# Two decode layers on one core: the last half row of the second up projection in two loads, and nine idle products less

## The chip, the cores and the metric

The kernel runs on 1 core of one Trainium2 chip. The metric is the device time of one execution in microseconds (us); the kernel before takes 2681.52 us, median of 3 runs (2681.52 to 2681.58). The names of the engines are those of the profile: PE multiplies matrices (PEld loads its stationary operand), DVE, ACT and POOL work on vectors, SP does nothing here but issue transfers, and 16 DMA engines carry them from the memory into `space`, the one large buffer on the core. Idle products are matmuls whose results nobody reads; they only keep PE occupied.

## The reference

Two tokens (B = 2) go through the same attention block and the same gated MLP twice. Cut to what matters:

```python
def _A_ref(x, k_cache, v_cache, wq, wo):           # H = 32 heads of 128, 8192 cached keys, all float32
    q = (x @ wq).reshape(B, 1, H, 128).transpose(0, 2, 1, 3)
    p = softmax(einsum("bhqd,bhkd->bhqk", q, k_cache) * 128 ** -0.5)
    o = einsum("bhqk,bhkd->bhqd", p, v_cache)
    return o.transpose(0, 2, 1, 3).reshape(B, 1, H * 128) @ wo      # wo: 4096 x 576
def _B_ref(x, w_gate, w_up, w_down):               # 576 -> 4608 -> 576
    h = gelu(x @ w_gate) * (x @ w_up)
    return h @ w_down
x = A_x
for _ in range(2):
    x = x + _A_ref(layernorm(x), A_k_cache, A_v_cache, A_wq, A_wo)
    x = x + _B_ref(layernorm(x), B_w_gate, B_w_up, B_w_down)
```

The caches are 268 MB each and are read once for each layer; a few units stay on the core between the layers.

## The kernel before, in words

**Order of the loads.** `plan_first`, `plan_mlp(0)`, `plan_second` and `plan_mlp(1)` put every load of the program into one list, and `pump` issues them in that order on SP as soon as the place in `space` that a load wants is free. A load is freed by `done(key)` after the last instruction that reads it. So SP's queue has one fixed order, and a load that waits for its place holds back all behind it.

**Attention** walks over 34 items (two heads of one token, or one head at the end): DVE multiplies keys and query, POOL and DVE add up, ACT takes the exponentials, PE multiplies with the values. Layer 1 walks backwards over the items, so that what lies on the core at the end of layer 0 is used first. At the end of an attention `project(g)` multiplies with pieces of `wo`.

**MLP.** In layer 0 (`split`) the three weights come in pieces of 1152 KB through a ring of four places (`RING`, `NPLACE`), each piece multiplied by `split_products` or by the loop over `DOWN` and freed at once. In layer 1 they come in few large pieces that are put wherever there is room (`Arena.fit`). There a weight of 576 x 4608 is looked at as 1152 half rows of 2304 numbers (9216 bytes); partition p holds the half rows 9p to 9p + 8, and half row number `u` of every partition is called the `u`-th. `half_rows` loads a range of `u` for all 128 partitions. `GU` says which ranges make a load: gate 0 to 4 and 5 to 8, up 0 to 5 and 6 to 8. The ninth half row is `u` = 8.

**The matching x.** `norm` turns the normalised x into `xt`: 32 columns for each `u`, of which two, at `PAD + 32 * u`, hold x for the full row, and the two behind them hold x for the other half; the rest is zero. `window(u, at)` takes eight columns, so that a product of eight columns lands gate and up, and both halves, in rows of their own in `acc`. `all_products` multiplies: for each `u` two halves of the columns and four groups, eight matmuls, each of 288 columns. In float32 the profile shows each matmul as two.

**Behind it** `activate` (ACT and DVE) makes gelu(gate) * up, the loop over `DOWN[1]` multiplies with the five pieces of `w_down`, `add_to_x` adds, and two transfers store x.

**Idle products.** `idle_products(n, side)` writes matmuls of the identity into a part of PSUM that is free just then: two of 128 columns without a side and for n = 1, one of 512 columns with a side and n = 2. `IDLE` gives their numbers ahead of each piece of `DOWN`; others stand between the pieces of `wo` at the end of the first attention.

Of the kernel before, what the change touches and what calls it, by code (L numbers as in the profile page):

```python
# [15 lines left out]
P = 128  # L16
B = 2
# [8 lines left out]
HALF = P // 2  # L26
# [3 lines left out]
NU = 9  # L30
EQ = 512
HG = DF // 16
PAD = 6
NT = 4
NI = DF // (NT * P)
CW = D // 4
# [89 lines left out]
def decode_layers(ctx, tc, x_in, kc, vc, wq, wo, wg, wu, wd, out):  # L126
    nc = tc.nc
# [21 lines left out]
    queue, ready, places = [], {}, {}  # L149
# [5 lines left out]
    def done(key):  # L155
        arena.free(key)
        pump()
# [93 lines left out]
    def half_rows(key, w, us, first):  # L251

        width = w.shape[1] // 2
        rows = w.rearrange("r (s w) -> (r s) w", w=width).rearrange("(p u) w -> p u w", p=P)

        def transfers(t):
            nc.sync.dma_start(t.rearrange("p (u w) -> p u w", w=width), rows[:, us[0]:us[-1] + 1, :])

        weights(key, len(us) * width, first, transfers)

    def of_half(h, k):

        width = wq.shape[1] // 2
        rows = wq.rearrange("r (s w) -> (r s) w", w=width).rearrange("(m u) w -> m u w", u=2 * NU)
        first, step = (2 * k + h, NU + 1 - 2 * h)

        def transfers(t):
            nc.sync.dma_start(t, rows[:, first:first + step + 1:step, :])

        weights(("wq", 1, h, k), width, None, transfers)  # L270
# [54 lines left out]


    single = [range(u, u + 1) for u in range(NU)]
    GU = [[range(0, 5), range(5, NU)], [range(0, 6), range(6, NU)]]

    DOWN = [  # L330
        [[(h, lo, lo + 4)] for h in range(2) for lo in range(0, 16, 4)] + [[(h, 16, 18) for h in range(2)]],
        [[(0, 0, 18)]] + [[(1, lo, hi)] for lo, hi in ((0, 9), (9, 15), (15, 17), (17, 18))],
    ]

    IDLE = [(0, 0, 2, 0, 2, 0, 2, 0, 0), (10, 2, 2)]

    whole_at = (None, 0)
    def groups(layer):
        return range(H // WIDE[layer])[::1 - 2 * layer]
# [76 lines left out]
    def plan_mlp(layer):  # L416
        if layer == 0:
            for h in range(2):
                for u in range(4):
                    split_rows("g", wg, h, u)  # L420
                for u in range(4):
                    split_rows("u", wu, h, u)
                if h == 0:
                    split_ninth("g", wg)
                    split_ninth("u", wu)
        else:
            for g, (name, w) in enumerate((("g", wg), ("u", wu))):
                for us in GU[g]:
                    half_rows((name, layer, us[0]), w, us, 0)
        for piece in DOWN[layer]:  # L430
            down(layer, piece)

# [99 lines left out]
    def small(p, n):  # L532

        if n > 2:
            return turned[0:p, 0:n]
        return pair[0:p, 0:n]
# [50 lines left out]
    def idle_products(n, side=None):  # L587
        wide = P if side is None else 4 * P if n % 2 == 0 else 2 * P
        to = turned if side is None else acc[:, side, :wide]
        for _ in range(2 * P * n // wide):  # L590
            nc.tensor.matmul(
                to[0:4, :], ident[:, 0:4], ident.unsqueeze(1).to_broadcast([P, wide // P, P]), start=True, stop=True
            )
# [13 lines left out]
    def attention(layer):  # L607
# [30 lines left out]
        else:  # L638
            half_products(1)
            key = ("wq", 1, NU - 1)  # L640
# [434 lines left out]
        if layer == 0:  # L1075
            project(second)

            third, fourth, fifth = groups(layer)[2:5]
            values(N - 1, 0, 2)
            for g in (third, fourth):  # L1080
                project(g)
                idle_products(1)
            for k in range(2, ITEMS[n].parts, 2):
                values(N - 1, k, k + 2)
                if k + 2 == ITEMS[n].parts:
                    nc.scalar.copy(back, spare)
                idle_products(1)
            gather(n)
            project(fifth)
            idle_products(1)  # L1090
            context(n)
            divide(n)
        else:
            values(N - 1)
            finish(n)
            regroup()
        spread()
        for g in groups(layer)[5:] if layer == 0 else groups(layer):
            project(g)
            if layer == 0 and g != groups(layer)[-1]:  # L1100
                idle_products(1)
        add_to_x()


    def mlp(layer):
# [10 lines left out]
        def split_products(h):  # L1116
# [3 lines left out]
            for key, u, g in steps:  # L1120
# [10 lines left out]
                if key != steps[-1][0]:  # L1131
                    idle_products(1, 1 - h if (u < 4 if h == 0 else u) else None)

        def all_products():

            for g, name in enumerate("gu"):
                for us in GU[g]:
                    w = ready.pop((name, layer, us[0])).rearrange("p (u c m v i) -> p u v c m i", m=32, v=2, c=4, i=NI)
                    for u in us:
                        for v in range(2):  # L1140
                            for c in range(4):
                                nc.tensor.matmul(
                                    acc[32 * c:32 * c + 4 * B, v, :HG], window(u, 4 * g), w[:, u - us[0], v, c],
                                    start=(g == 0 and u == 0), stop=(g == 1 and u == NU - 1),
                                )
                    done((name, layer, us[0]))

        def activate(v):

# [19 lines left out]
                nc.vector.scalar_tensor_tensor(to[:, :, s, :], a, 1.0, by, op0=ALU.add, op1=ALU.mult)  # L1169

        if not split:
            all_products()
        for v in range(2):
            if split:
# [54 lines left out]
```

## Time and profile before

| what | us |
|---|---|
| median of 3 runs | 2681.52 |
| the profiled execution's own time | 2681.31 |
| its span, first to last instruction | 2679.5 |
| PE, DVE, POOL, ACT busy | 880.8, 1992.6, 1560.5, 165.7 |
| bytes read | 1152.39 MB, 430 GB/s over the span |

The 1.8 us between the span and the execution's time lie outside all instructions. Layer 0 ends at about 1367 us of the span, layer 1 takes the rest. A window row gives, for a stretch of the span, the busy time of the engines with the number of their instructions, the granted share of PE's clock, the mean busy share of the 16 DMA engines and the rate at which they moved bytes. (A share may be a little over 1, since a packet of an engine starts a few ns before the one ahead of it has ended.) In the chain of waits each row is a start, a length and what the program waited for.

### The profile page before, as it was taken

Reading aid. Unit: us, or ns where it says so; the run is one execution under the profiler, and the core shown is the slowest. Engines: PE = TensorE matmul, PEld = TensorE weight load, DVE = VectorE, ACT = ScalarE, POOL = GpSimd, SP = SyncE. Lnnn points to the kernel's source line nnn. Section 1 sums busy time; section 2 is a strip of 40 time slices with the busy share of each in tenths; the row PEclk is TensorE's granted clock in tenths of the full one; section 3 lists DMA queues with packets and bytes.
Section 4 is the critical chain, followed back from the end, with each engine's and each line's share of the span. In section 5 each row is a group of like instructions: output and inputs, shape, how many; then the busy total and the mean of one; then the engine's idle time right before and its main releaser. Section 6 shows DMA issues by size and latency. Waiting matters only on the chain.

```text
span 2679.5 us, 15405 instructions
## 1 busy us (share of the span) xinstructions
PE 880.8 (33%) x6198; PEld 268.7 (10%) x6198; DVE 1992.6 (74%) x907; ACT 165.7 (6%) x792; POOL 1560.5 (58%) x411
## 2 busy tenths in 40 slices
PE   1313332232223233334663323223222323332346
PEld 0000000000000000011221000000000000000022
DVE  4877888888788888867038778888888888888740
ACT  0000000000000000001026000000000000000000
POOL 2546676667667666744028457666766666676620
PEclk8666655665665566566986665566566556655678
DMA  9999999999999999999999999999999999999998
GB/s 423 437 429 434 436 434 432 431 436 433 431 434 434 434 433 432 436 428 427 417 417 431 436 433 434 434 430 434 435 432 432 436 434 433 431 437 434 428 430 385
DMA packets 29207, 1153.39 MB, mean 430 GB/s; under 512 B 3256, under 2 KB 3280, under 8 KB 4048
## 3 DMA queue, kind: packets, MB, share of 16 engines
q1 hardware_dynamic: 29096, 1152.40, 99.8%
q8 instruction: 48, 0.79, 0.1%
q14 instruction: 23, 0.19, 0.0%
q10 hardware_dynamic: 40, 0.01, 0.0%
HBM read 1152.39 MB, written 0.00 MB: 430 GB/s over the span
## 4 chain that ended last, share of the span: by engine, by line
DMA 67%; DVE 19%; PE 8%; POOL 2%; ACT 2%; issue 1%; another core or an unknown queue 0%; SPq 0%; POOLq 0%; ACTq 0%; DVEq 0%
DMA space<-in_A_k_cache_dram 59%; DVE space L743 17%; PE acc L891 3%; DMA space<-in_B_w_down_dram 2%; DMA space<-in_B_w_gate_dram 2%; POOL space L772 2%; DVE scores L775 2%; PE bank L658 1%; DMA space<-in_A_v_cache_dram 1%; DMA space<-in_B_w_up_dram 1%; PE bank L809 1%; ACT prz L832 1%; PE acc L913 1%; DMA space<-in_A_wo_dram 1%; PE bank L845 1%
## 5 line engine op out<-in xcount | busy, mean ns | idle before, releaser
L772 POOL TENSOR_TENSOR space<-space 128x3072 f32<-128x3072 f32 (+4 forms) x221 | 1128.4, 5106 | 459.1 <-DVE space L743 330.7
L743 DVE TENSOR_TENSOR space<-space,bank 128x6144 f32<-128x6144 f32 (+4 forms) x223 | 1111.9, 4987 | 344.7 <-DMA space<-in_A_k_cache_dram 273.7
L775 DVE TENSOR_REDUCE scores<-space 128x48 f32<-128x3072 f32 (+4 forms) x223 | 568.7, 2550 | 92.1 <-POOL space L772 92.1
L913 PE MATMUL acc<-space,prz 128*16 128x512 f32 (+1 forms) x3312 | 510.1, 780 | 357.9 <-DMA space<-in_A_v_cache_dram 346.4
L883 POOL TENSOR_TENSOR space<-space 128x2048 f32<-128x2048 f32 x147 | 398.0, 2708 | 392.3 <-DVE space L880 376.8
L658 PE MATMUL bank<-qsb,few 4*64 4x128 f32 (+1 forms) x256 | 46.1, 436 | 894.8 <-DVE space L743 887.1
L880 DVE TENSOR_TENSOR space<-space,bank 128x4096 f32<-128x4096 f32 x49 | 216.6, 4421 | 1.7
L913 PEld LDWEIGHTS acc<-space,prz 128*16 128x16 f32 (+1 forms) x3312 | 108.7, 117 | 742.0 <-issue 449.7
L824 ACT ACTIVATE nbs<-bank 128x2 f32<-128x2 f32 (+1 forms) x68 | 11.6, 171 | 2010.4 <-PE bank L809 1957.1
L658 PEld LDWEIGHTS bank<-qsb,few 4*64 4x64 f32 (+1 forms) x256 | 20.6, 201 | 914.2 <-DVE space L743 897.4
L580 POOL TENSOR_TENSOR rstd<-ve,few 128x1 f32<-128x1 f32 x4 | 2.2, 551 | 171.3 <-DVE ve L578 171.3
L891 PE MATMUL acc<-space,few 128*16 128x512 f32 x98 | 92.6, 1048 | 0.0
L801 PE MATMUL bank<-ident,m 128*1 128x128 f32 x68 | 20.7, 305 | 196.1 <-DVE m L799 195.9
L936 PE MATMUL bank<-few,wide 128*32 128x4 f32 (+1 forms) x272 | 20.9, 200 | 170.1 <-DVE wide L928 170.1
L1153 DVE STREAM_TRANSPOSE gu<-acc 128x288 f32<-128x288 f32 x4 | 1.9, 484 | 92.6 <-ACT acc L1151 92.6
L832 ACT ACTIVATE prz<-scores,nbs 64x128 f32<-64x128 f32 (+1 forms) x128 | 50.7, 396 | 11.7 <-POOL prz L822 8.9
L765 ACT ACTIVATE space<-space 128x128 f32<-128x128 f32 x164 | 48.4, 297 | 19.5 <-DVE space L743 16.5
L809 PE MATMUL bank<-m,few 1*128 1x2 f32 (+1 forms) x136 | 39.0, 353 | 28.1 <-DVE m L807 28.1
L584 DVE TENSOR_TENSOR x<-bank,x 128x144 f32<-128x144 f32 x4 | 1.2, 308 | 59.4 <-PE bank L1186 39.7
L927 DVE TENSOR_TENSOR acc<-acc,few 128x512 f32<-128x512 f32 x34 | 23.5, 691 | 29.2 <-PE acc L913 29.2
L936 PEld LDWEIGHTS bank<-few,wide 128*32 128x32 f32 x272 | 19.1, 154 | 216.0 <-issue 211.0
L955 ACT ACTIVATE oT<-bank,rinv 32x8 f32<-32x8 f32 x108 | 28.1, 260 | 190.1 <-PE bank L936 189.1
(105 smaller groups left out, 495.8 us busy)
## 6 DMA issues: line engine op xcount, KB each, us to landing
space<-in_A_v_cache_dram SPq DMA_DIRECT2D x7, 4096.0 KB
space<-in_A_k_cache_dram SPq DMA_DIRECT2D x6, 4096.0 KB
space<-in_B_w_gate_dram SPq DMA_DIRECT2D x9, 1152.0 KB
space<-in_B_w_up_dram SPq DMA_DIRECT2D x9, 1152.0 KB
space<-in_B_w_down_dram SPq DMA_DIRECT2D x8, 1152.0 KB
space<-in_A_wq_dram SPq DMA_DIRECT2D x9, 1024.0 KB
space<-in_A_wo_dram SPq DMA_DIRECT2D x2, 4608.0 KB
space<-in_A_k_cache_dram SPq DMA_DIRECT2D x4, 2048.0 KB
```

What stands on the lines that cost most here:

```text
L658: nc.tensor.matmul(qb[n][to, :], pick[32 * c:32 * c + 4, r:r + 1].to_broadcast([4, P // it.heads]), qsb[32 * c:32 * c + 4, (h % 4) * DH:(h ...
L743: nc.vector.tensor_tensor(out=u[:, :r, :], in0=t[:, :r, :], in1=qb[n].unsqueeze(1).to_broadcast([P, r, DH]), op=ALU.mult)
L765: nc.scalar.activation(u[:, j, :], u[:, j, :], AF.Copy, accum_out=S[n][:, base(n, k) + j:base(n, k) + j + 1])
L772: nc.gpsimd.tensor_tensor(out=half, in0=half, in1=u[:, :r, DH // 2:], op=ALU.add)
L775: nc.vector.tensor_reduce(out=S[n][:, base(n, k):base(n, k) + own_rows(n, k, m)], in_=prod.pop((n, k)), axis=AX.X, op=ALU.add)
L809: nc.tensor.matmul(mT[n][:, :heads], ones[0:1, :], m1[:, :heads], start=True, stop=True)
L832: nc.scalar.activation(pr[at, lo:].rearrange("p (g e) -> p g e", e=4)[:, 0:it.rows // 2 * it.heads:2 * it.heads, :], s[at, :it.rows].rearr ...
L880: nc.vector.tensor_tensor(out=t, in0=t, in1=share.unsqueeze(2).to_broadcast([P, rows, DH]), op=ALU.mult)
L883: nc.gpsimd.tensor_tensor(out=t[:, :rows - less], in0=t[:, :rows - less], in1=t[:, less:rows], op=ALU.add)
L891: nc.tensor.matmul(accumulator(n)[0:16, :], owner[:, 8 * ITEMS[n].b:8 * ITEMS[n].b + 16], part_at(arena.live[key, lo][0], 4 * DH), start=F ...
L913: nc.tensor.matmul(accumulator(n)[32 * c:32 * c + m, :], pr[:, at:at + m], t[g // 4][:, g % 4 * 4:g % 4 * 4 + 4, :].rearrange("p j d -> p ...
L936: nc.tensor.matmul(po[lo:lo + 32, i, :c], t[:, i::GH], of[:, :c], start=True, stop=True)
```

## The change

The ninth half rows of the second layer's up weight no longer come with the range 6 to 8. They come in two loads of 64 half rows each, behind the range 0 to 5. The half rows of the even partitions go to their own partitions, 0, 2, 4 and so on. Those of the odd partitions go to partitions 0 to 63, in a column range beside: the source is written as 8 x 8 rows with the outer step over `g`, so that row `j * 8 + g` of the 64 lands on partition `g * 8 + j`. To fit this, `spread_ninth` makes a permutation matrix from the identity (ACT), multiplies it with the ninth columns of `xt` (PE), and puts the permuted and the remaining x into unused zero columns of the ninth block (ACT). `ninth_products` multiplies both loads: eight matmuls over 128 partitions and eight over 64, instead of eight over 128. Nine idle products fall away: six of 128 columns at the end of the first attention and three of 512 columns ahead of pieces of the first `w_down`.

```diff
+NINTH = PAD + 32 * (NU - 1)
...
+    def ninth_rows(key, w):
+
+        width = w.shape[1] // 2
+        rows = w.rearrange("r (s w) -> (r s) w", w=width).rearrange("(q e u) w -> e q u w", e=2, u=NU)[:, :, NU - 1, :]
+        lower = rows[1].rearrange("(j g) w -> g j w", g=8)
+
+        def transfers(t):
+            nc.sync.dma_start(t[0:P:2, :width], rows[0])
+            nc.sync.dma_start(t[:HALF, width:], lower)
+
+        weights(key, 2 * width, 0, transfers)
...
-    GU = [[range(0, 5), range(5, NU)], [range(0, 6), range(6, NU)]]
+    GU = [[range(0, 5), range(5, NU)], [range(0, 6), range(6, NU - 1)]]
...
-    IDLE = [(0, 0, 2, 0, 2, 0, 2, 0, 0), (10, 2, 2)]
+    IDLE = [(), (10, 2, 2)]
...
             project(fifth)
-            idle_products(1)
             context(n)
...
         for g in groups(layer)[5:] if layer == 0 else groups(layer):
             project(g)
-            if layer == 0 and g != groups(layer)[-1]:
-                idle_products(1)
...
+        def spread_ninth():
+
+            perm = scores[:, :HALF]
+            nc.scalar.copy(
+                perm.rearrange("p (g j) -> p g j", g=8), ident.rearrange("p (j g e) -> p e g j", g=8, e=2)[:, 1]
+            )
+            moved = small(HALF, 2 * B)
+            nc.tensor.matmul(moved, perm, xt[:, NINTH:NINTH + 2 * B], start=True, stop=True)
+            nc.scalar.copy(xt[:HALF, NINTH + 24:NINTH + 24 + 2 * B], moved)
+            nc.scalar.copy(xt[:, NINTH + 12:NINTH + 12 + B], xt[:, NINTH:NINTH + B])
+
+        def ninth_products():
+
+            w = ready.pop(("u", layer, NU - 1)).rearrange("p (u c m v i) -> p u v c m i", m=32, v=2, c=4, i=NI)
+            for at, p in ((NINTH + 12, P), (NINTH + 24, HALF)):
+                for v in range(2):
+                    for c in range(4):
+                        nc.tensor.matmul(
+                            acc[32 * c:32 * c + 4 * B, v, :HG], xt[:p, at - 2 * B:at + 2 * B], w[:p, p == HALF, v, c],
+                            start=False, stop=False,
+                        )
+            done(("u", layer, NU - 1))
...
         if not split:
+            spread_ninth()
             all_products()
```

On SP, at the end of the second layer, the loads stand so before, a row with its partitions and the numbers in each:

```order
L320 DMA space<-in_A_wo_dram 128x9216 x2
L257 DMA space<-in_B_w_gate_dram 128x11520
L257 DMA space<-in_B_w_gate_dram 128x9216
L257 DMA space<-in_B_w_up_dram 128x13824
L257 DMA space<-in_B_w_up_dram 128x6912
L297 DMA space<-in_B_w_down_dram 128x10368
```

and now so:

```order
L258 DMA space<-in_B_w_gate_dram 128x9216
L258 DMA space<-in_B_w_up_dram 128x13824
L269 DMA space<-in_B_w_up_dram 64x2304
L270 DMA space<-in_B_w_up_dram 64x1x2304
L258 DMA space<-in_B_w_up_dram 128x4608
L310 DMA space<-in_B_w_down_dram 128x10368
```

The load of 128 x 6912 has become one of 128 x 4608 behind two of 64 x 2304; nothing passes anything else. (Line numbers differ because the file grew.)

On PE, in the second MLP, from the layer norm (`apart`) to the first piece of `w_down` (`hT`), before:

```order
L547 MATMUL bank_124<-apart,wide 128x24
L1142 MATMUL acc<-space,xt 8x288 x144
L591 MATMUL acc<-ident 4x512 x5
L1186 MATMUL bank<-space,hT 4x144 x72
L591 MATMUL acc<-ident 4x512
```

and now:

```order
L562 MATMUL bank_124<-apart,wide 128x24
L1153 MATMUL bank_124<-xt,scores 64x4
L1177 MATMUL acc<-space,xt 8x288 x120
L1163 MATMUL acc<-space,xt 8x288 x16
L1177 MATMUL acc<-space,xt 8x288 x16
L606 MATMUL acc<-ident 4x512 x5
```

One permuting product stands ahead, and sixteen products with the ninth half rows stand where eight stood, now ahead of the half rows 6 and 7.

On PE, in the first layer, from the last products with `w_up` (`xt`) over the first `w_down` (`hT`) to the norm of the second layer, before:

```order
L1125 MATMUL acc<-space,xt 8x288 x8
L1186 MATMUL bank<-space,hT 4x144 x32
L591 MATMUL acc<-ident 4x512
L1186 MATMUL bank<-space,hT 4x144 x32
L591 MATMUL acc<-ident 4x512
```

and now:

```order
L606 MATMUL acc<-ident 4x256
L1137 MATMUL acc<-space,xt 8x288 x8
L1224 MATMUL bank<-space,hT 4x144 x144
L606 MATMUL acc<-ident 4x256
L562 MATMUL bank_124<-apart,wide 128x24
```

The first lists the beginning of this `w_down`, with two of the three idle products in it; in the second all 144 matmuls of the nine pieces stand in one row. At the end of the first attention the same happens to the pieces of `wo`: the six idle matmuls between them are gone, and the real products stand in the same order.

More of the change, by code (lines that the diff above doesn't have):

```diff
@@ L429, in plan_mlp @@
                     half_rows((name, layer, us[0]), w, us, 0)
+                    if (g, us[0]) == (1, 0):
+                        ninth_rows((name, layer, NU - 1), w)
         for piece in DOWN[layer]:
@@ L1143, in all_products @@
                                     acc[32 * c:32 * c + 4 * B, v, :HG], window(u, 4 * g), w[:, u - us[0], v, c],
-                                    start=(g == 0 and u == 0), stop=(g == 1 and u == NU - 1),
+                                    start=(g == 0 and u == 0), stop=(g == 1 and u == NU - 2),
                                 )
                     done((name, layer, us[0]))
+                    if (g, us[0]) == (1, 0):
+                        ninth_products()
         def activate(v):
```

## The prediction

> **What bounds the kernel.** I read the page first, then the end of the chain of waits, then the last microseconds in windows.
>
> ```profile
> PE 880.8 (33%) x6198; PEld 268.7 (10%) x6198; DVE 1992.6 (74%) x907; ACT 165.7 (6%) x792; POOL 1560.5 (58%) x411
> ...
> DMA packets 29207, 1153.39 MB, mean 430 GB/s; under 512 B 3256, under 2 KB 3280, under 8 KB 4048
> ...
> 2622.76 46.63 DMA space<-in_B_w_down_dram
> ...
> 2669.43 2.39 PE bank L1186 x72
> ...
> 2673.56 2.57 PE bank L1186 x72
> ...
> 2676.16 0.31 DVE x L584
> ```
>
> No compute engine is busy for more than 74%. The DMA engines carry 430 GB/s over the whole span, and the chain ends with a load of `w_down` that waited 46.6 us behind other loads. So the end is set by when the last DMA engine has carried its share; PE follows within a microsecond. The question is whether all 16 end together:
>
> ```profile
> 2670.00:2670.50 0.50, 0.50 (x24) 1.00 1.03 424
> 2670.50:2671.00 0.50, 0.50 (x24) 1.00 0.84 346
> 2671.00:2671.50 0.50, 0.50 (x24) 1.00 0.65 272
> 2671.50:2672.00 0.50, 0.50 (x13) 1.00 0.60 253
> 2672.00:2672.50 0.50, 0.50 (x2) 1.00 0.54 221
> 2672.50:2673.00 0.50, 0.16 (x1) 1.00 0.71 268
> 2673.00:2673.50 0.50, 0.00 (x0) 1.00 0.53 217
> 2673.50:2674.00 0.50, 0.44 (x16) 1.00 0.40 161
> 2674.00:2674.50 0.50, 0.50 (x24) 1.00 0.46 180
> 2674.50:2675.00 0.50, 0.50 (x24) 1.00 0.18 69
> 2675.00:2675.50 0.50, 0.50 (x23) 1.00 0.01 5
> ```
>
> These are PE's windows; the last two numbers are the DMA share and the rate. They do not end together. The share falls like a staircase from 2670.5 to about 2675.1 (0.01 of the last window on 16 engines is 0.08 us on one). Times 16 it counts the engines still at work: 10 in the window from 2671.0, 8.5 in that from 2673.0, 6.4 in that from 2673.5. The sum of the ten shares from 2670.5 on is 4.92; times 0.5 us the mean engine ends 2.46 us after 2670.5, at 2672.96. Perfect balance would thus save 2675.1 - 2673.0 = 2.1 us, 0.08% of the time. No way of dealing out the same bytes at the end can save more.
>
> **The two loads.** The ninth half rows are 128 packets of 9216 bytes. Before, as part of 128 rows, each of 16 engines carries 8 of them. How a load of fewer rows is dealt out, the start and the whole program show (first 100 us, then the page):
>
> ```profile
> q10 hardware_dynamic: 32, 0.01, 0.0%
> ...
> x<-in_A_x_dram ACTq DMA_DIRECT2D x8, 1.1 KB
> ...
> q1 hardware_dynamic: 29096, 1152.40, 99.8%
> ```
>
> Eight loads of two rows make 32 packets: 16 rows, and two closing packets for each load, so each row had an engine of its own. SP's 202 loads of 128 rows and one store of four make 29096 = 202 x (128 + 16) + 8 packets: sixteen engines for 128 rows, four for four. A load thus spreads over up to 16 engines by its outer count. That of the even half rows (outer 64) should go to 16, four rows each. That of the odd ones is written with an outer count of 8 and should go to 8, eight rows each. Then eight engines carry 12 rows and eight carry 4, where all carried 8: four rows, 36.9 KB, are moved from each of one half to each of the other. At 431 GB/s (below), 26.9 for one engine, that is 1.37 us later for one half and 1.37 us earlier for the other. Eight engines also get 8 smaller packets for 8 large ones. The price of more packets is bounded by two stretches, small packets in the first, 64 KB in the second:
>
> ```profile
> 1250.00:1370.00 120.00, 78.52 (x1061) 32.39 (x1061) 20.17 (x47) 3.35 (x12) 7.35 (x7) 0.91 1.01 419
> ...
> 2480.00:2580.00 100.00, 32.23 (x193) 0.62 1.00 431
> ```
>
> 9216 bytes take 352 ns at 419/16 and 342 ns at 431/16, so at most 10 ns for a packet, 0.1 us for eight and the closing ones.
>
> Whether 1.37 us is gained or lost depends on which half is late. Of that I know only this: something delays single engines.
>
> ```profile
> q8 instruction: 7, 0.11, 0.5%
> ```
>
> In the last 100 us seven packets of instructions, 16 KB each, took 0.5% of 1600 engine-us: 8 us, 1.1 us for each, every one on one engine. Four on one engine and none on another make the staircase. No view names engines; the packets followed from end to start put these fetches on eight engines alone, and the two that load x at the start are not among them. If the eight of the odd load are the first eight, as those two would be, the late half is relieved. I take that.
>
> Then the late half ends at 2675.1 - 1.37 = 2673.7. The early half ended by about 2673.5, where the count falls below eight, and ends at 2674.9 at most now. So the early half sets the new end: a gain of 0.2 us at the row's edge, 0.7 us if its last engine was done at 2673.0. The count there is still 8.5, so I stay near the edge: 0.3 us, less 0.1 us for the packets, 0.2 us. Both ends are kept: -1.4 us if the early half is earlier than the rows let it seem, +1.5 us if the late half gets the bytes.
>
> [...]
>
> **Work that is added in the second MLP**, all of it beside transfers:
>
> ```profile
> 2608.44 0.69 DVE L574 STREAM_TRANSPOSE xt<-xc 128x288 f32<-128x288 f32 x1
> ...
> 2615.62 7.11 PE L1142 MATMUL acc<-space,xt 128*8 128x288 f32 x80 [8.08 <-DMA space<-in_B_w_gate_dram]
> ...
> 2642.79 11.60 PE L1142 MATMUL acc<-space,xt 128*8 128x288 f32 x144 [10.58 <-DMA space<-in_B_w_up_dram]
> ...
> 2654.52 0.47 ACT L1151 ACTIVATE acc<-acc,rstd 128x288 f32<-128x288 f32 x1 [80.27 <-PE acc L1142]
> ...
> 2657.39 5.86 PE L591 MATMUL acc<-ident 128*4 128x512 f32 x10 [3.00 <-DVE gu L1153]
> ...
> 2669.43 2.39 PE L1186 MATMUL bank<-space,hT 128*4 128x144 f32 x72 [0.74 <-DMA space<-in_B_w_down_dram]
> ...
> 2620.62 8.28 SPq L297 DMA_DIRECT2D space<-in_B_w_down_dram  x5
> ```
>
> The permutation is three ACT copies (0.47 us each at most, by the far larger row) and one PE product: 1.5 us with hand-overs. ACT idles 80 us there, the first copy needs nothing of the norm, and PE waits 8.08 us for the gate weight, 6.5 us of it after `xt` is there at 2609.1. Cost nothing; with that cover gone, 1.5 us. Eight more matmuls show as 16; at 11.60/144 = 81 ns that is 1.3 us. They push `activate` and the 5.86 us of idle products back, and the first products with `w_down` by as much; ahead of the second piece PE idles 0.74 us behind another 1.02 us of idle products, which is the cover. Cost nothing; without the cover 1.3 us. The larger place for the ninth rows makes the third to fifth `w_down` pieces wait for the second gate load's products (about 2632) in place of the first's (2622.8). On the way to the end they have 30 us and more of loads ahead of them (46.63 above), so nothing. Two more issues on SP come at 2604, behind which nothing waits.
>
> **The nine idle products** sit among pieces of 1152 KB:
>
> ```profile
> 1346.64 2.10 PE L1186 MATMUL bank<-space,hT 128*4 128x144 f32 x32 [1.50 <-DMA space<-in_B_w_down_dram]
> ...
> 1353.18 1.02 PE L591 MATMUL acc<-ident 128*4 128x512 f32 x2
> ...
> 1355.10 1.16 PE L1186 MATMUL bank<-space,hT 128*4 128x144 f32 x32 [0.89 <-DMA space<-in_B_w_down_dram]
> ...
> 1357.80 1.16 PE L1186 MATMUL bank<-space,hT 128*4 128x144 f32 x32 [1.54 <-DMA space<-in_B_w_down_dram]
> ...
> 1353.43 9.88 DMA space<-in_B_w_down_dram
> ```
>
> The pieces land every 2.70 us (1355.10 to 1357.80). Real products take 1.16 us of it, so the 1.02 us removed only lengthen waits: gain nothing. They may let PE's clock fall; the row at 1346.64 shows the same products at their slowest, 2.10 us, still inside 2.70. A place is then freed 0.9 us later; the load issued at 1353.43 took 9.88 us, 7 of them in the queue. That is the cover, and the DMA share of 1.01 over this stretch says that no engine runs dry. Cost nothing; with the queue empty, 0.9 us for each piece.
>
> PE's count stays: 18 records less, 16 + 2 more. So the instruction fetches at the end stay in phase.
>
> **Sum:** -0.3 + 0.1 = -0.2 us. The profiled execution (2681.31, of it 2679.5 span) would be 2681.1; the median lies 0.2 above it, so 2681.3.
>
> **Rivals.**
> - The whole gain: the early half has room, the end goes by the late half alone: -1.3 us, 2680.2. Against it stands 8.5 engines at 2673.0. 0.10.
> - The bytes go to late engines (the fetches are not where I think): +1.5 us, 2683.0. For it: no row names engines. 0.19. [...]
> - The change doesn't do what it says: the odd load goes to 16 engines after all, all keep 8 rows, 2681.6. Against it the packet counts. 0.08.
> - Slower by more than 0.2%: the load falls to very few engines, since its partition side (64) and source side (8) disagree. On k engines each carries 64/k rows of 0.342 us beside its four, where it had eight: +4.1 us at k = 4, of which the early half absorbs 1.6; +9.6 us at k = 2; +20.5 us at k = 1. It decides from k = 2 on, with a time of 2689 to 2700. Against it: two and four rows took as many engines. 0.03.
> - PE's clock starves the ring: 0.9 us for each of nine pieces, 8 us, less the queue of 7: +1 us, 2682.5. 0.05, of which 0.01 for a ring that stays empty so long that 5.4 us are lost.
>
> My own case has 0.54, and a gain from something that no row shows 0.01. A measurement of this kernel can tell about 0.2% (5.4 us) from no change. Faster by that much would need more than perfect balance: 0.01. Slower: 0.03 for the few engines and 0.01 for the ring. Within: 0.95. The range goes from the whole gain to the bytes on late engines, 2680.0 to 2683.2, which leaves out the few-engine case and oddities.
>
> **What will show it.** In the profile after: 29096 + 152 = 29248 packets on SP's queue if the odd load is on eight engines, eight more if on 16; a staircase at the end that is shorter, its foot 0.2 us earlier; PE records 6198; PE still waiting for `w_down` three times at the end; a DMA share of 1.01 from 1250 to 1370. I am wrong if the foot moves out by 1.4 us, or if the share falls anywhere before 2670.

## The result, and the profile after

The changed kernel takes 2694.91 us (median of 6 runs, 2692.49 to 2696.11) against 2681.52: 13.4 us more by the medians, a ratio of the means of 1.0048 with a 95% interval of 1.0037 to 1.0059. The profiled execution took 2692.49 us, its span 2690.7. I had forecast 2681.3.

The page of the changed kernel first: PE's instructions, and SP's queue with its packets.

```profile
PE 880.9 (33%) x6198; PEld 270.5 (10%) x6198; DVE 1992.5 (74%) x907; ACT 166.1 (6%) x795; POOL 1560.2 (58%) x411
...
q1 hardware_dynamic: 29248, 1152.40, 99.5%
```

Both counts are those that were forecast: 29248 packets stand for an odd rows' load on eight engines (in the trace eight landings raise that load's semaphore, sixteen that of the even rows), and PE has as many records as before. The difference is in the timeline of PE and SP (start, duration, engine, line; in brackets how long the engine idled before and what ended that).

```profile
2599.91 0.50 SPq L269 DMA_DIRECT2D space<-in_B_w_up_dram  x1
...
2608.89 0.35 PE L1153 MATMUL bank<-xt,scores 128*64 128x4 f32 x2 [1.73 <-DVE ve L593]
...
2645.30 17.99 PE L1177 MATMUL acc<-space,xt 128*8 128x288 f32 x240 [36.06 <-DMA space<-in_B_w_up_dram]
...
2651.68 4.52 SPq L310 DMA_DIRECT2D space<-in_B_w_down_dram  x5
```

L1177 at 2645.30 is the first product of the second MLP, with gate row 0. It needs the first gate load and `xt`. Before (the row at 2615.62 in the prediction), it started at 2615.62, after 8.08 us of waiting for that gate load. Now it waits 36.06 us, and what it waits for is a load of `w_up`. All the gate products and the products with up rows 0 to 5 then run in one piece, and the `w_down` loads, which need the places of the gate weight, are issued at 2651.68 in place of 2620.62. The chain of waits says the same (start, length, what was waited for):

```profile
2593.18 6.72 PE bank L981 x127
2599.91 45.26 DMA space<-in_B_w_up_dram
2645.30 17.99 PE acc L1177 x228
2663.29 2.21 PE acc L1163 x32
2665.50 2.25 PE acc L1177 x32
...
2670.98 5.00 PE acc L606 x9
```

The load on it was issued at 2599.91. That is L269, the even ninth half rows. From its landing on the chain is compute to the end, 42 us. In it are 5.00 us of idle products (L606), which before lay ahead of the products that went by the landing of `w_down`. Before, the chain ended with 46.63 us of a `w_down` load.

The order of the changed program shows the wait (an output of the compiled order, where a name such as DMAHW4 is the semaphore of one load); first the line of before, then that of after:

```
L1142 MATMUL acc<-space,xt 8x288 [waits DMAHW1_49,DVE_49,Pool_49]
L1177 MATMUL acc<-space,xt 8x288 [waits DMAHW4_49,DMAHW1_49,Pool_49]
```

DMAHW1 is the first gate load. DMAHW4 is the even ninth load, whose place (by the program's plan numbers 23040 to 27648 of each partition) does not touch that of the gate weight (34816 to 46336). The trace has both semaphores: the gate load had landed whole at 2615.24, the even ninth load at 2645.17, and the product began at 2645.30. So the dependence is a false one: the product reads nothing that the load writes. The load's destination, `t[0:P:2, :width]`, is the only one here with a step over the partitions.

The rates show a second thing. PE's windows of the changed kernel (busy PE, PE's clock, DMA share, GB/s), then those of before:

```profile
2638.00:2648.00 10.00, 2.70 (x24) 0.50 0.92 294
2648.00:2655.00 7.00, 7.00 (x100) 0.88 0.68 238
```

```profile
2638.00:2648.00 10.00, 5.21 (x56) 0.57 0.98 422
2648.00:2655.00 7.00, 6.39 (x96) 1.00 1.03 439
```

From 2648 the share drops to 0.68: the queue has run empty, since `w_down` is issued late. From 2638 to 2648 it is different: the engines are busy for 0.92 of the time and yet move 294 GB/s, where 422 come at 0.98. They are busy and slow.

### The profile page after: what moved, and what is told of

Same layout as the page of the kernel before. It is cut to its first block, busy times and chain, and to the rows that moved or that the text cites. A ratio compares the mean times of both kernels' runs of the same rounds, so it can differ in the third digit from the quotient of the medians.

```text
span 2690.7 us, 15413 instructions
## 1 busy us (share of the span) xinstructions
PE 880.9 (33%) x6198; PEld 270.5 (10%) x6198; DVE 1992.5 (74%) x907; ACT 166.1 (6%) x795; POOL 1560.2 (58%) x411
## 3 DMA queue, kind: packets, MB, share of 16 engines
q1 hardware_dynamic: 29248, 1152.40, 99.5%
## 4 chain that ended last, share of the span: by engine, by line
DMA 67%; DVE 18%; PE 9%; POOL 2%; ACT 2%; issue 1%; SPq 0%; POOLq 0%; DVEq 0%; ACTq 0%
DMA space<-in_A_k_cache_dram 60%; DVE space L758 16%; PE acc L906 3%; DMA space<-in_B_w_up_dram 3%; DMA space<-in_A_v_cache_dram 3%; POOL space L787 2%; DVE scores L790 2%; PE bank L673 1%; PE bank L824 1%; ACT prz L847 1%; PE acc L1177 1%; DMA space<-in_B_w_down_dram 1%; PE bank L1224 1%; PE bank L860 1%; DMA space<-in_A_wo_dram 1%
## 5 line engine op out<-in xcount | busy, mean ns | idle before, releaser
L774 POOL TENSOR_TENSOR space<-space,qs 128x512 f32<-128x512 f32 x23 | 29.3, 1274 | 18.0 <-ACT qs L755 18.0
```

## The experiments

The theory from the first traces: the step over the partitions makes the false wait, the gate products come late, with them the places for `w_down`, and the queue runs dry; that is the whole loss. Its rivals: the load on eight engines, the permutation and the doubled products of the ninth row, the missing idle products, or simply the cutting of one load into several.

Each run has its own runs of the kernel before on the same chip; the differences in us are of the medians, the ratios of the means.

| run | wait for a stepped load until | time, us | against before, us | ratio, 95% interval |
|---|---|---|---|---|
| the change | 2645.30 | 2694.91 | +13.4 | 1.0037 to 1.0059 |
| even and odd places | 2645.79 | 2691.52 | +10.1 | 1.0024 to 1.0054 |
| two halves | none | 2689.49 | +8.0 | 1.0019 to 1.0041 |
| odd low, even high | none | 2689.89 | +8.4 | 1.0020 to 1.0043 |
| ninth first | 2631.11 | 2688.45 | +7.0 | 1.0015 to 1.0034 |
| even and odd places, ninth first | 2630.03 | 2682.13 | +0.3 | 0.9991 to 1.0010 |
| odd on sixteen | 2648.50 | 2696.25 | +14.4 | 1.0037 to 1.0067 |
| eight engines, stepped, first | 2635.09 | 2688.51 | +6.7 | 1.0014 to 1.0034 |
| key cache in halves | none | 2705.14 | +23.3 | 1.0072 to 1.0102 |
| key cache in steps | none | 2681.81 | 0.0 | 0.9991 to 1.0010 |
| two loads of 32, first | 2632.98 | 2690.21 | +8.4 | 1.0019 to 1.0039 |
| two loads of 32 | 2649.42 | 2696.40 | +14.6 | 1.0040 to 1.0070 |
| eight own, first | 2627.66 | 2683.55 | +2.0 | 0.9999 to 1.0017 |
| eight far, first | 2632.88 | 2689.38 | +7.9 | 1.0017 to 1.0040 |
| no idle products | none | 2681.76 | 0.0 | 0.9992 to 1.0010 |

### The wait, with and without a step

Even and odd places, from the kernel before: the ninth half row gets a load pair and a place of its own.

```diff
+        rows = w.rearrange("r (s w) -> (r s) w", w=width).rearrange("(q u) w -> q u w", u=NU)[:, NU - 1, :]
...
+            nc.sync.dma_start(t[0:P:2], rows[0:P:2])
+            nc.sync.dma_start(t[1:P:2], rows[1:P:2])
```

> The kernel before, with its ninth up half rows as a load of their own into a place of 2304 numbers in a partition: the even rows to partitions 0, 2, ... and the odd ones to 1, 3, ..., each load 64 rows on 16 engines. No permutation, no load on eight engines, the idle products are there, the products are those of before (eight of the ninth row, before rows 6 and 7). Theory (a wait on the destination with a partition step of 2: the first gate product waits for these loads, the gate places come free some 30 us late, w_down is issued late and the DMA queue runs dry): first gate product waits until about 2645, w_down issued at about 2651, time 2693 to 2696, as the changed kernel. Rival 1 (the load on eight engines costs the time): none is here, 2681.5. Rival 2 (the missing idle products cost it): they are here, 2681.5. Rival 3 (the permutation and the doubled products hold PE up): neither is here, 2681.5.

Two halves, the same without a step:

```diff
-            nc.sync.dma_start(t[0:P:2], rows[0:P:2])
-            nc.sync.dma_start(t[1:P:2], rows[1:P:2])
+            nc.sync.dma_start(t[:HALF], rows[:HALF])
+            nc.sync.dma_start(t[HALF:], rows[HALF:])
```

> As the run with even and odd places, with one difference: the first 64 of the rows go to partitions 0 to 63 and the last 64 to partitions 64 to 127, so neither destination has a step. Same number of loads, bytes, products and the same place. Theory (only the step makes the wait): the first gate product waits about 8 us for its gate weight as before, w_down is issued at about 2621, time 2681.5 within 0.8. Rival (two loads more on the queue, or the ninth row as a place of its own, cost the time): 2693 to 2696 like the other.

First the run with even and odd places, timeline and windows of PE, then that with two halves:

```profile
2645.79 17.70 PE L1165 MATMUL acc<-space,xt 128*8 128x288 f32 x240 [38.15 <-DMA space<-in_B_w_up_dram]
...
2674.79 0.42 PE L1211 MATMUL bank<-space,hT 128*4 128x144 f32 x6
```

```profile
2650.00:2651.00 1.00, 1.00 (x24) 1.00 0.06 16
```

```profile
2615.24 7.33 PE L1165 MATMUL acc<-space,xt 128*8 128x288 f32 x80 [8.18 <-DMA space<-in_B_w_gate_dram]
```

```profile
2640.00:2650.00 10.00, 3.20 (x28) 0.50 0.98 223
```

The step makes the wait, as the theory had it: with it the first product waits 38.15 us and the time is 10.1 us longer, without an eight-engine load, a permutation or a missing idle product anywhere. Without the step the wait is gone. But the theory had said 2681.5 for that run, and it took 2689.49. Its loss is of the second kind: ten microseconds at a share of 0.98 with only 223 GB/s.

One part of the theory falls here. The queue does run dry in the first run (a share of 0.06 at 2650), but no product with `w_down` waits for its weight: the row at 2674.79 and all behind it have no idle time before them. What costs the time is that PE starts late. The 72 gate products (144 records), which ran in the shade of the up loads before, now stand behind the wait, on the path to the end.

### Removing the step from the change, and shortening the wait

Odd low, even high:

```diff
-            nc.sync.dma_start(t[0:P:2, :width], rows[0])
-            nc.sync.dma_start(t[:HALF, width:], lower)
+            nc.sync.dma_start(t[HALF:, :], rows[0])
+            nc.sync.dma_start(t[:HALF, :], lower)
...
```

> The changed kernel, but the even ninth half rows go to partitions 64 to 127 in a row and the odd ones to 0 to 63, on eight engines as in the change; the permutation puts xt into that order for all 128 rows at once, and the ninth row takes eight products of 128 partitions in place of sixteen. The nine idle products are left out as in the change. Theory (the wait alone makes the loss): no wait at 2609 beyond the gate load's, w_down issued at about 2621, time 2681.3, the number that the prediction gave for the change: within 2680.0 and 2683.2. Rival 1 (eight engines carry twelve rows and become the last): 2683.0. Rival 2 (a load on eight engines or the missing idle products cost 13 us): 2693 to 2696.

Ninth first:

```diff
+                    if (g, us[0]) == (1, 0):
+                        ninth_rows((name, layer, NU - 1), w)
                     half_rows((name, layer, us[0]), w, us, 0)
-                    if (g, us[0]) == (1, 0):
-                        ninth_rows((name, layer, NU - 1), w)
```

> The changed kernel with its two ninth loads put ahead of the load of up rows 0 to 5 (7.1 MB, about 16.5 us of transfers), all else as in the change. Theory (the first gate product waits for the even ninth load, wherever that stands): it waits until about 2628.5 in place of 2645.3; w_down is issued at about 2635 with some 14 us of up loads still queued, so the queue doesn't run dry and the time is 2681.5 within 1.5. Rival 1 (the load on eight engines costs it, in any place): 2693 to 2696. Rival 2 (the wait alone matters, not the empty queue behind it: whatever PE loses there is lost at the end): half of the wait is left, some 2688.

Both missed by 7 to 9 us, and both show the slow transfers again. A row and a window of the run with odd low, even high:

```profile
2616.58 7.11 PE L1182 MATMUL acc<-space,xt 128*8 128x288 f32 x80 [6.04 <-DMA space<-in_B_w_gate_dram]
...
2640.00:2650.00 10.00, 0.00 (x0) 0.53 0.89 194
```

Without the step the first product waits 6.04 us for its gate weight and the first `w_down` load is issued at 2621.55, and still the time is 2689.89. So the wait is one cause and there is another, in all of these runs but that with even and odd places. What separates that one is where the rows go: before its queue ran empty it moved at full rate (416 GB/s at a share of 0.98 from 2638 to 2645).

The other corner of the square is then: a short wait, and even and odd places.

> The run with even and odd places, with its two ninth loads put ahead of the load of up rows 0 to 5. Theory (two causes, the wait and the shared partitions): this has neither, since the wait ends some 17 us earlier, before the queue runs dry, and the even and odd places moved at full rate; time 2681.8, within 2681.0 and 2684; the first gate product waits until about 2630; the share stays near 1.0 with 410 GB/s or more from 2600 to 2660. Rival (a ninth row as a place and loads of its own costs 7 to 8 us whatever its partitions, as the runs with two halves, with odd low and even high, and with the ninth first agree within 1.5 us): 2688 to 2690.

The windows of the run with the ninth first, then of this one, with PE's rows of both:

```profile
2623.00:2633.00 10.00, 1.90 (x18) 0.50 1.06 287
```

```profile
2623.00:2633.00 10.00, 2.97 (x28) 0.50 1.05 450
```

```profile
2631.11 11.64 PE L1177 MATMUL acc<-space,xt 128*8 128x288 f32 x144 [22.11 <-DMA space<-in_B_w_up_dram]
2652.63 8.12 PE L1177 MATMUL acc<-space,xt 128*8 128x288 f32 x96 [9.89 <-DMA space<-in_B_w_up_dram]
```

```profile
2630.03 10.87 PE L1165 MATMUL acc<-space,xt 128*8 128x288 f32 x144 [20.46 <-DMA space<-in_B_w_up_dram]
2646.29 8.19 PE L1165 MATMUL acc<-space,xt 128*8 128x288 f32 x96 [5.39 <-DMA space<-in_B_w_up_dram]
```

The wait of 20 us is there in both, and in the second it costs nothing: 2682.13, a ratio of 1.0000. So the second rival of the run with the ninth first, which had named 2688 for the halved wait, had the number and not the cause. A wait until 2630 still hides behind the up loads, one until 2645 doesn't. The rate is the other cause: 287 against 450 GB/s over the same ten microseconds, the up rows 0 to 5 land 6.3 us later (2652.63 against 2646.29), and the time is 6.3 us longer. With the four corners: wait alone +10.1, rate alone +7.0, both +13.4, neither +0.3. The corner of the rate also has the change's load on eight engines and its doubled products; the run with eight own, first (below) has these too, at full rate, and takes +2.0, so about 5 of the 7.0 us are the rate. The two causes don't add up. In the profiled execution of the change, its fastest, PE starts no later (2645.30) than with even and odd places (2645.79), and the span is only 1.0 us longer. In the profiles of odd on sixteen and of two loads of 32 it starts at 2648.50 and 2649.42, and these runs take +14.4 and +14.6. So where the wait is there, slow transfers show as far as they put off the landing on which PE waits; that this makes the spread of the change's own six runs (2692.49 to 2696.11) is not shown.

### The rate alone, in the middle of the program

Key cache in halves, from the kernel before; one load of 8.39 MB (128 rows of 65536 bytes) in the second attention becomes two of 4.19 MB:

```diff
+            if key == ("k", 1, 20):
+                t = part_at(at[0], parts * PART).rearrange("p (j d) -> p j d", d=DH)
+                s = ITEMS[n].source(src)
+                nc.sync.dma_start(t[:HALF], s[:HALF, 0:parts * JC, :])
+                nc.sync.dma_start(t[HALF:], s[HALF:, 0:parts * JC, :])
+            else:
+                load(at[0], n, src, 0, parts)
-            load(at[0], n, src, 0, parts)
```

> The kernel before, all of it, with one load of 4 MB of the key cache in the middle of the second attention split into two loads of 64 rows: rows 0 to 63 to partitions 0 to 63, then rows 64 to 127 to 64 to 127, each on 16 engines. The same bytes, products and order; the product that reads it waits for both. Theory (16 engines that write into 64 neighbouring partitions get half the rate): 4.19 MB take 19.5 us in place of 9.75, so 9.7 us are lost, time about 2691, within 2688 to 2693; the share stays at 1.0 and the rate falls to some 215 GB/s for about 20 us. Rival (no such thing in the middle, the loss is of the end and of the small packets alone): 2681.5.

Key cache in steps has `0:P:2` and `1:P:2` in place of the two halves.

> As the run with the key cache in two halves, but the two loads take the even rows to partitions 0, 2, ... and the odd rows to 1, 3, ...; on every engine the instructions wait for the same things as in that run. Theory (only which partitions an engine writes decides the rate): no loss, 2681.5 within 0.8. Rival (two loads of 64 rows cost the time, whatever partitions they go to): the same loss as in the other run.

PE's windows of the first and of the second:

```profile
1742.00:1788.00 46.00, 7.33 (x49) 0.57 0.98 203
1790.00:1836.00 46.00, 12.91 (x71) 0.57 1.00 433
```

```profile
1742.00:1788.00 46.00, 14.83 (x85) 0.57 1.00 434
1790.00:1836.00 46.00, 13.76 (x80) 0.64 1.00 434
```

Same bytes, same packets, same waits, and 23.3 us against nothing. What differs is which 64 rows make a load, and with that the partitions that they go to; the next section holds the source rows fixed. The size was off by a slip: 9.7 us had been expected for 4.19 MB at half rate, but that is one half, and both halves are slow. 8.39 MB take 41 us at 203 GB/s and 19 at 434, which is 22 of the 23.3 us. The transfer records agree: 144 packets of 65536 bytes take more than 3.5 us, 5.1 in the median in place of 2.42; the load itself has 128.

Steps of two show no false wait among the cache loads: 2681.81 us, 0.0 against before. Why the dependence is drawn in the MLP and not there was not tried.

### Which engine may write where

Odd on sixteen undoes the eight engines of the change and leaves all else:

```diff
-        lower = rows[1].rearrange("(j g) w -> g j w", g=8)
+        lower = rows[1]
...
```

> The change with one part undone: the odd rows' load goes to partitions 0 to 63 on sixteen engines, four rows each, instead of eight with eight rows each (the permutation only packs the odd rows). Theory (packed partitions make the half rate, on eight engines or sixteen, and the wait stays): 2694 to 2697, as the change. Rival (the load on eight engines is one of the causes): 2691.5, as the run that has the wait alone.

Eight engines, stepped, takes the run with even and odd places first, and puts the odd rows on eight engines:

```diff
-            nc.sync.dma_start(t[1:P:2], rows[1:P:2])
+            nc.sync.dma_start(t[1:P:2], lower)
...
```

> As the run with even and odd places loaded first, with the odd rows' load on eight engines (its source counted 8 by 8, as in the change) into partitions 1, 3, ..., a permutation of xt to that order, and without the nine idle products. It asks what eight engines cost when no partitions 0 to 63 are packed. Theory (packed partitions make the half rate, the number of engines doesn't): as the run before within the 1.5 us that the prediction gave for the moved bytes. Rival (each engine of the eight writes rows that lie among those of two others, which costs the rate as well): 2687 to 2691.

A window of each, odd on sixteen first:

```profile
2640.00:2650.00 10.00, 1.50 (x16) 0.50 0.96 225
```

```profile
2620.00:2630.00 10.00, 0.00 (x0) 0.50 1.08 309
```

With sixteen engines in partitions 0 to 63 the time is that of the change (2696.25). Its two ninth loads read the same source rows as those with even and odd places; only the odd rows' destination differs, and their 128 packets of 9216 bytes take 605 ns in the median, against 351 there. So it is not the source rows. With eight engines in steps the time is 2688.51, so there the rival was right: packing alone doesn't explain it, eight engines are slow in spread-out partitions too (309 GB/s). One explanation, an assumption: in a load of 128 rows each engine has partitions of its own, and an engine that writes another's halves the rate of both. Four runs tried that. Two loads of 32, first, and the same at the place of the change, against the change:

```diff
-        lower = rows[1].rearrange("(j g) w -> g j w", g=8)
+        lower = rows[1].rearrange("(b g j) w -> b g j w", b=2, g=8)
...
-            nc.sync.dma_start(t[:HALF, width:], lower)
+            for b in range(2):
+                nc.sync.dma_start(t[32 * b:32 * b + 32, width:], lower[b])
...
```

> The run with the ninth loads ahead (the first gate product then waits only until about 2629), with one more edit: the 64 odd rows go to partitions 0 to 63 by two loads of 32 rows in place of one of 64, each on eight engines, four rows an engine. So each engine writes the four partitions (of 0 to 31, then of 32 to 63) that are its own in a load of 128 rows, if four consecutive rows go to an engine there. New theory: besides the wait, the transfers themselves run at half rate while two engines write into each other's partitions (the run with two halves, which has no such wait, moved 223 GB/s at a DMA share of 0.98 from 2640 to 2650). By it this kernel has neither loss: 2681.5, within 2680.0 and 2684, the share at 2620 to 2640 near 1.0 with 415 GB/s or more. Rival (the half rate comes from 64 or fewer rows to a load, or from packets of 9216 bytes, or from a load on eight engines): it stays at 2688.5 or is longer, with three small loads in place of two.

> The changed kernel with the odd rows in two loads of 32 rows, as in the run before, the ninth loads at the place of the change. The wait for the even ninth load stays, the shared partitions are gone. Theory (two losses, the wait and the half rate): as the run with even and odd places, which has the wait alone: 2691.5, within 1.5; the DMA share dips below 0.4 about 2650, the windows from 2638 to 2646 carry 400 GB/s or more. Rival (one loss only): 2694.9 as the change, or 2681.5.

Eight own, first, against two loads of 32, first:

```diff
-        lower = rows[1].rearrange("(b g j) w -> b g j w", b=2, g=8)
+        lower = rows[1].rearrange("(b j g) w -> b g j w", b=2, g=8)
...
```

> The earlier run with own places did not do what it was to do: 29272 packets on SP's queue mean that its two loads of 32 rows went to sixteen engines, two rows each. Here the source of each is counted 8 by 4 in another order, so that it goes to eight engines with four rows each (29256 packets), to partitions 4g to 4g+3 of the first or the second 32 for engine g; the permutation follows. All else as in the run with the ninth loads first: the wait is short. Model 1 (in a load of 128 rows an engine writes four partitions of one 32 and four of the next; eight engines with eight rows in a row put two engines on the same partitions' way): each of the eight now writes where it always does, no half rate, 2682.0, within 2680.5 and 2684, with the moved bytes in it (by the prediction -0.2 or +1.5). Model 2 (an engine's own partitions are eight neighbours): two engines share them, half rate, 2686 to 2690.

Eight far, first, against eight own, first:

```diff
-                nc.sync.dma_start(t[32 * b:32 * b + 32, width:], lower[b])
+                nc.sync.dma_start(t[HALF + 32 * b:HALF + 32 * b + 32, width:], lower[b])
...
```

> As the run before, with one difference: the same two loads of 32 rows on eight engines go to partitions 64 to 127 (the products read them there, the permutation follows). Model 1: the eight engines now write what eight other engines write, half rate as long as those carry other loads, 2685 to 2690. Rival (the number of rows that lie together decides, not whose partitions they are): the same time as the run before, whichever that is.

The first pair told nothing of engines that stay in their own partitions. The loads went to sixteen engines, as the page's packets show (29256 would be eight); that the counts of 8 and 4, whose source rows lie one behind the other, were merged into 32 is a guess. Both runs kept the half rate (+8.4 and +14.6).

```profile
q1 hardware_dynamic: 29272, 1152.40, 99.6%
```

The second pair did what it was to do. Windows of the run with eight own, then of that with eight far:

```profile
2620.00:2630.00 10.00, 2.34 (x20) 0.50 1.04 446
2630.00:2640.00 10.00, 8.56 (x128) 0.98 1.01 433
```

```profile
2620.00:2630.00 10.00, 0.00 (x0) 0.50 1.07 271
2630.00:2640.00 10.00, 7.12 (x92) 0.72 0.98 370
```

The same two loads on the same number of engines run at 446 GB/s into partitions 0 to 63, and at 271 into 64 to 127. In the transfer records the 128 packets of 9216 bytes take 351 ns in the median and at most 360 in the first, 692 and up to 748 in the second. The loads beside them are slowed too: of the 128 packets of up rows 0 to 5 (55296 bytes, 2.05 us in the median in both) 24 take more than 2.55 us in the second, up to 4.06, and one in the first. Rows, order and number of engines are the same, so the destination decides. An engine's own partitions would explain it; the records name no partition and no engine.

Both times fall where Model 1 had put them: 2683.55 in 2680.5 to 2684, and 2689.38 in 2685 to 2690. Model 2 had 2686 to 2690 for the first. Which partitions are an engine's own no record shows, so the model stays an assumption that fits the times. That in the change's own load two engines meet on the same partitions is part of it and was not measured by itself.

One run doesn't fit as simply. In the run with even and odd places sixteen engines carry 64 rows with a step of two. If they were dealt four in a row, an engine would span eight neighbouring partitions, not Model 1's four, and yet all 128 packets took 347 to 359 ns. How they are dealt no run shows, so the explanation stays open there.

### The idle products

```diff
-    IDLE = [(0, 0, 2, 0, 2, 0, 2, 0, 0), (10, 2, 2)]
+    IDLE = [(), (10, 2, 2)]
```

and the six between pieces of `wo`, in the kernel before.

> The kernel before without the nine idle products, and nothing else of the change. Theory, and the prediction's step (the products lie in waits for pieces that land every 2.70 us): 2681.5 within 0.8. Rival (PE's clock falls without them and pieces are freed late): 2682.5 to 2687.

2681.76, a ratio of 1.0001. PE's window over that stretch, in this run and then in the changed kernel:

```profile
1250.00:1370.00 120.00, 76.92 (x1044) 0.89 1.00 417
```

```profile
1250.00:1370.00 120.00, 80.99 (x1043) 0.84 1.01 418
```

PE's clock was 0.91 before; it is 0.89 here and 0.84 in the change, and the transfers don't notice (419, 417 and 418 GB/s).

## Why the prediction was wrong

**The step that failed** is in the paragraph on the work added in the second MLP, "Cost nothing" and "Two more issues on SP come at 2604, behind which nothing waits". It took for granted that the first gate product waits for its gate weight alone. I looked for what the added loads would make SP wait for and not for who would wait for them. The first gate product waits for the even ninth load, 36.06 us in place of 8.08. This alone is 10.1 us (even and odd places). The 72 gate products, hidden before, stand on the path. With that the opening step falls too, that the end is set by the last DMA engine and PE follows: the last 42 us of the chain are compute, and no product waits for `w_down`.

**The eight added matmuls** were to cost nothing, or 1.3 us without the cover. The cover was gone: the ninth products take 2.42 us in 32 records, against 1.30 in 16 with even and odd places, on the path to the end.

**"So nothing" for the later w_down pieces** falls with it. The third to fifth were to come at about 2632 behind 30 us of queued loads. All five were issued from 2651.68 on, with the queue run down. That by itself did not show at the end, since PE was later still.

**The two loads** were counted right and priced wrong. 29248 packets: eight engines, as the row of small loads and the packet counts had said. But the price of a packet of 9216 bytes, 342 to 352 ns, was taken from loads of 128 rows, and it was assumed to hold wherever a row lands. In the changed kernel the 128 packets of the ninth rows take 429 ns in the median and up to 740, and neighbours on the queue are slowed as well (of the packets of 55296 bytes the longest takes 3.12 us, before 2.50). The argument went over 36.9 KB on this or that half, 1.37 us; the term that was missing is about 5 us (ninth first, +7.0, against eight own, first, +2.0, which differ in the odd rows' places and in their coming in two loads).

**The moved bytes** themselves, over which the prediction weighed -0.2 against +1.5, no run shows. Nor does any run show that the odd load's eight engines are those of the early half, from which the -0.3 of the sum came; shown is that they are eight (29248 packets). The run with eight own, first moves them and takes +2.0 us (0.9999 to 1.0017, that is -0.3 to +4.6), but there the end goes by PE:

```profile
2646.73 8.38 PE L1180 MATMUL acc<-space,xt 128*8 128x288 f32 x96 [8.17 <-DMA space<-in_B_w_up_dram]
2654.91 2.40 PE L1166 MATMUL acc<-space,xt 128*8 128x288 f32 x32
```

From the landing ahead of 2646.73 on the chain is compute to the end, and no product waits for `w_down`. So which half of the engines is late stays open. The count of engines in the staircase is rough as well: its share rises twice on the way down (0.54 to 0.71, 0.40 to 0.46).

**Right** were the idle products (1.0001 without them), the hidden permutation (its product ran at 2608.89), and PE's 6198 records. A slowdown of more than 5.4 us had been given a chance of 0.04. The rival of the few engines named a time of 2689 to 2700, into which the result falls, but by another mechanism: the load was on eight engines and not on two.

**The sign to watch** that the text gave, a share that falls anywhere before 2670, is what the trace shows (0.68 from 2648 to 2655), though the empty queue was not what cost the time. It would have missed the second cause, in which the share stays near 1 and only the rate falls.

## What to carry to other kernels

When a load is added or cut up, look in the compiled order for who now waits for it, the readers of other places in the same buffer too, above all where the destination has a step over the partitions (here the first gate product waited 36.06 and 38.15 us with one, 6.04 and 8.18 without; among the cache loads a step cost nothing); here a false wait cost nothing as long as other loads hid it (+0.3 us for a start at 2630.03), and cost time once work that had been hidden stood behind it (10.1 us for a start 30 us later than before). Mind which partitions a cut load goes to: here 64 rows on sixteen engines packed into 64 neighbouring partitions ran at about half rate (203 GB/s against 434 in the cache load; 605 ns against 351 for a packet of the ninth rows), in steps of two at full rate, and eight engines at full rate in one set of places (446 GB/s) and slowly in the three others tried (294, 309 and 271). Judge a stretch by its rate and its share together: a share of 0.98 at 203 GB/s meant slow packets, not a full stream.

## What was not expected of the hardware

A load of 8.39 MB in two packed halves ran at 203 GB/s and cost 23.3 us, while the same load in even and odd partitions cost nothing (1.0001). Splitting by partition was thus free or very dear here for the same number of loads, packets and bytes. Of the versions tried none beats the kernel before: the best of those that cut out the ninth row, even and odd places with the ninth first, equals it at 1.0000 with an interval of 0.9991 to 1.0010.
